# Two unused tiles of 32 bytes that move x, the activations and the weights in SBUF

## The chip, the cores and the metric

The kernel runs on one core of one Trainium2 chip. The metric is the device time in microseconds of one execution. Three timed executions of the kernel before took 531.8, 532.85 and 533.78 us; their median is 532.85 us.

## What is computed

Two steps follow each other: a gated linear attention, and a feed-forward layer with an own activation.

```python
# q, k, v, f_logit: (4, 8, 768, 48) float32
f = 1.0 / (1.0 + np.exp(-f_logit))
state = zeros((B, H, D, D))
for t in range(S):
    state = f[:, :, t, :, None] * state + einsum('bhd,bhe->bhde', k[:, :, t], v[:, :, t])
    y[:, :, t] = einsum('bhd,bhde->bhe', q[:, :, t], state)
x = y.transpose(0, 2, 1, 3).reshape(B * S, H * D)      # 3072 x 384
h = x @ w_in                                           # w_in: 384 x 2048
g = np.where(h >= 1, h, np.where(h <= -1, 0.0, (h + 1) ** 2 / 4.0))
out = g @ w_out                                        # w_out: 2048 x 384
```

## The kernel before, in words

The 768 steps of time are cut into six blocks of 128. In a block the 4 batches lie side by side, so a block has 512 columns. The eight heads are taken as four pairs; a pair of heads lies on 112 of the 128 partitions.

**Attention.** For each block and pair, VectorE builds the running products of the gates with scans and multiplies them into k and q (tile `kq`). TensorE makes the scores (line 411), VectorE masks them (line 417, tile `am`), and TensorE makes the outputs (lines 460 to 465: `am` and `v`, and from the second block on `kq` and the decayed state `dbd`) and the new state (line 493). These matmuls have float32 operands and 128 or 48 columns. ScalarE and VectorE split each output y into a rounded part and the rest, both in the 4-byte type float32r (lines 472 and 473), which is tile `x`: two buffers, one for blocks 0, 2, 4 and one for blocks 1, 3, 5, each of 128 partitions with 2 parts of 3 slices of 512 columns. The rows of the fourth pair go through tile `y3` and small DMAs into `x`.

**Feed-forward layer.** It runs in 96 units: six blocks times 16 slices of 128 of the 2048 inner columns. A unit has three stages:
- nine matmuls of 128x128 weights on 512 columns into PSUM tile `ph` (line 198, function `mm_in`): for each of three slices of x, low weights on the rounded x, high weights on the rounded x, high weights on the rest of x;
- the activation: ScalarE (lines 202 and 205), VectorE (line 210), then its split into `ghi` (ScalarE, line 213) and `glo` (VectorE, line 216);
- nine matmuls into the three PSUM tiles `po` (line 222, function `mm_out`): low weights on `ghi` and high weights on `ghi` for each of three output slices, and then high weights on `glo`.

So there are 1728 matmuls of 512 float32r columns. In each, x, `ghi` or `glo` is the moving operand, which streams through the array, and a slice of `w_hi` or `w_lo` is the stationary operand, which a LDWEIGHTS loads before it. The profile shows the two on rows of their own, PE for the matmul and PEld for the weight load, and the load for the next matmul lies beside the present one.

**Weights.** They come from HBM as 24 pieces of 512 KB (tile `raw`), and in the first 130 us VectorE and ScalarE turn each into a high and a low float32 part (lines 291 to 304, tiles `bits`, `w_hi`, `w_lo`). They stay in SBUF from then on.

**What sets the order.** A planner in the file (class `Plan`) takes every operation with an engine, a cost from a table and what it depends on, simulates the engines and gives out the instructions in the order of the simulated start times. It also puts bf16 matmuls on a tile of zeros (line 272) where it sees TensorE idle for long. Nothing in it knows of addresses.

**Where tiles lie.** All tiles come from one pool with one buffer each. They stand in SBUF in the order in which the code asks for them, each rounded up to a multiple of 32 bytes per partition. Most tiles are a multiple of 64 bytes long; `f`, `kq`, `act` and the small ones are an odd multiple of 32. In the built program before, `x_0` begins at byte 65920 of each partition, `x_1` at 78208, `ghi_0` at 98752, `glo_0` at 102848, `w_hi` at 127424 and `w_lo` at 176576. All six are multiples of 64. Every slice of x that a matmul streams begins a multiple of 2048 bytes further on, every slice of weights a multiple of 512.

Of the kernel before, what the change touches and what calls it, by code (L numbers as in the profile page):

```python
# [10 lines left out]
F32 = mybir.dt.float32  # L11
# [121 lines left out]
def gla_moe(ctx: ExitStack, tc: tile.TileContext, ff, kqd, f0, vv, wd, maskd, identd, gates, values, headsd, out):  # L133
    nc = tc.nc
    const = ctx.enter_context(tc.tile_pool(name="const", bufs=1))
# [3 lines left out]
    def tiles(count, shape, dtype, name):  # L139
        return [const.tile(shape, dtype, name=f"{name}_{k}") for k in range(count)]  # L140
# [11 lines left out]
    kn = tiles(2, [C, B, C], F32, "kn")  # L152
    dbd = tiles(2, [R, B, R], F32, "dbd")
    state = const.tile([R, NP * B, D], F32, name="state")
    x = tiles(2, [128, 2, NP - 1, N], F32R, "x")
    y3 = const.tile([R, 2, N], F32R, name="y3")
    act_f = tiles(2, [128, N + 1], F32, "act")
# [2 lines left out]
    glo = tiles(2, [128, N], F32R, "glo")  # L160
    raw = tiles(4, [128, W], I64, "raw")
    bits = tiles(2, [128, W], U32, "bits")
    w_hi = const.tile([128, 2 * NW, W], F32R, name="w_hi")
    w_lo = const.tile([128, 2 * NW, W], F32R, name="w_lo")
    mask = const.tile([C, C], F32, name="mask")
# [570 lines left out]
```

## Time and profile before

| | |
|---|---|
| timed executions | 531.8, 532.85, 533.78 us (median 532.85) |
| the profiled execution's own time | 534.52 us |
| its span, from the first to the last instruction | 532.7 us |
| mean granted TensorE clock | 0.990 |
| TensorE matmuls busy | 516.1 us, 97% of the span |
| weight loads busy | 407.8 us, 77% |
| VectorE busy | 387.4 us, 73% |
| ScalarE busy | 275.3 us, 52% |
| DMA, mean rate | 78 GB/s |

The profile is one execution. Its views used here are: the page (busy times, the chain of work that ended last by engine and by line), that chain in order of time, the timeline of all instructions in a short window, and groups of instructions by line and shape (number, time in which at least one was running, mean duration of one in ns, idle time ahead of them). Matmuls overlap each other in the records, since one starts to stream while the one before it still drains; so the distance from one start to the next says what a matmul costs, and the mean duration of one is longer. A group in a window contains every instruction that was running in it, so a window of some tens of ns singles out one matmul.

### The profile page before, as it was taken

The page shows a single profiled execution, that of the slowest core. Times are in us where ns is not written, and L with a number is a line of the kernel's source. Part 1 is how long each engine was busy: PE and PEld are TensorE (multiplying, and loading weights), DVE is VectorE, ACT ScalarE, POOL GpSimd, SP SyncE. Part 2 cuts the span into 40 slices and gives each one's busy share as a digit, 9 for nine tenths or more (in the row PEclk, how much of TensorE's full clock was granted, in tenths as well). Part 3 has the DMA queues.
Part 4 walks back from the last instruction along what each step waited for, and adds up shares of the span by engine and source line. Part 5 has one row for each costly group of instructions (what it writes and reads, how often), then busy time and mean ns, then how long its engine had stood idle before and what let it go on. Part 6 is the DMA issues. An engine that isn't in the chain of part 4 may idle for free.

```text
span 532.7 us, 8347 instructions
## 1 busy us (share of the span) xinstructions
PE 516.1 (97%) x3265; PEld 407.8 (77%) x3272; DVE 387.4 (73%) x792; ACT 275.3 (52%) x447; POOL 2.6 (0%) x13
## 2 busy tenths in 40 slices
PE   9996999999999999999999999999999999999994
PEld 4554887778788888878888888888888887888883
DVE  6999899999999999999897697864444343433332
ACT  2589788997443443534534434434433434544442
POOL 1000000000000000000000000000000000000000
PEclk9997999999999999999999999999999999999998
DMA  8684353631332022312023221012300001100001
GB/s 297 207 297 167 120 182 133 218 115 30 95 94 65 19 76 56 99 54 75 22 74 52 84 72 58 1 55 42 93 16 0 2 0 31 61 0 0 1 0 63
DMA packets 18187, 41.67 MB, mean 78 GB/s; under 512 B 2976, under 2 KB 6560, under 8 KB 18144
## 3 DMA queue, kind: packets, MB, share of 16 engines
q1 hardware_dynamic: 18144, 41.09, 24.9%
q8 instruction: 27, 0.44, 0.3%
q14 instruction: 16, 0.13, 0.1%
HBM read 31.63 MB, written 4.72 MB: 68 GB/s over the span
## 4 chain that ended last, share of the span: by engine, by line
PE 78%; DVE 14%; ACT 4%; issue 2%; DMA 0%; SPq 0%; ACTq 0%; DVEq 0%
PE po L222 34%; PE ph L198 32%; PE pa L411 3%; PE pa L465 2%; PE pa L461 2%; PE ph L272 2%; DVE w_lo L304 2%; DVE bits L301 2%; DVE bits L294 1%; DVE act L210 1%; DVE am L417 1%; ACT raw L298 1%; DVE glo L216 1%; PE pa L460 1%; DVE kn L444 1%
## 5 line engine op out<-in xcount | busy, mean ns | idle before, releaser
L198 PE MATMUL ph<-x,w_hi 128*128 128x512 f32 x576 | 181.1, 395 | 0.0
L202 ACT ACTIVATE act<-ph,half 128x512 f32<-128x512 f32 x96 | 65.9, 687 | 151.0 <-PE ph L198 150.2
L198 PEld LDWEIGHTS ph<-x,w_hi 128*128 128x128 f32 x576 | 108.1, 188 | 25.9
L222 PE MATMUL po<-ghi,w_lo 128*128 128x512 f32 x288 | 116.6, 405 | 6.8 <-ACT ghi L213 6.7
L210 DVE SCALAR_TENSOR_TENSOR act<-ph,act 128x512 f32<-128x512 f32 x96 | 65.9, 687 | 75.2 <-ACT act L205 74.6
L198 PE MATMUL ph<-x,w_lo 128*128 128x512 f32 x288 | 114.1, 396 | 0.0
L222 PE MATMUL po<-ghi,w_hi 128*128 128x512 f32 x288 | 114.1, 396 | 0.0
L213 ACT CAST ghi<-act 128x512 fp32r<-128x512 f32 x96 | 59.4, 619 | 67.4 <-DVE act L210 66.9
L222 PE MATMUL po<-glo,w_hi 128*128 128x512 f32 x288 | 83.9, 393 | 0.1
L216 DVE TENSOR_TENSOR glo<-act,ghi 128x512 fp32r<-128x512 f32 x96 | 65.9, 686 | 22.0 <-ACT ghi L213 21.3
L222 PEld LDWEIGHTS po<-ghi,w_lo 128*128 128x128 f32 x288 | 54.4, 189 | 22.5 <-ACT ghi L213 9.2
L198 PEld LDWEIGHTS ph<-x,w_lo 128*128 128x128 f32 x288 | 54.2, 188 | 13.0
L222 PEld LDWEIGHTS po<-glo,w_hi 128*128 128x128 f32 x288 | 54.2, 189 | 12.8 <-DVE glo L216 1.0
L222 PEld LDWEIGHTS po<-ghi,w_hi 128*128 128x128 f32 x288 | 54.5, 189 | 11.9
L205 ACT ACTIVATE act<-act 128x512 f32<-128x512 f32 x96 | 60.7, 632 | 2.9
L444 DVE STREAM_TRANSPOSE kn<-kq 32x128 f32<-32x128 f32 x192 | 58.1, 303 | 2.9
L417 DVE TENSOR_TENSOR am<-pa,mask 128x512 f32<-128x512 f32 x43 | 29.2, 686 | 21.0 <-PE pa L411 17.8
L460 PE MATMUL pa<-am,v 128*64 128x128 f32 x184 | 35.2, 279 | 0.0
L461 PE MATMUL pa<-am,v 128*48 128x128 f32 x184 | 34.5, 276 | 0.1
L465 PE MATMUL pa<-kq,dbd 112*48 112x128 f32 x160 | 30.6, 272 | 0.0
L464 PE MATMUL pa<-kq,dbd 112*64 112x128 f32 x160 | 30.6, 272 | 0.0
L411 PEld LDWEIGHTS pa<-kq 48*128 48x128 f32 x344 | 21.3, 187 | 6.9 <-issue 6.3
(80 smaller groups left out, 478.2 us busy)
## 6 DMA issues: line engine op xcount, KB each, us to landing
raw<-in_w SPq DMA_DIRECT2D x24, 512.0 KB, 4.5
kq<-in_kq SPq DMA_DIRECT2D x18, 512.0 KB, 3.9
v<-in_v SPq DMA_DIRECT2D x24, 192.0 KB, 3.7
out_y<-raw SPq DMA_DIRECT2D x18, 256.0 KB, 2.2
f<-in_f SPq DMA_DIRECT2D x16, 256.5 KB, 2.8
kq<-kq SPq DMA_DIRECT2D x36, 64.2 KB, 2.3
x<-y SPq DMA_DIRECT2D x36, 64.0 KB, 2.3
act<-in_f SPq DMA_DIRECT2D x1, 256.5 KB, 5.5
```

The source lines that it names most:

```text
L198: nc.tensor.matmul(ps, w_in(part, j, kt), xt[:, t, kt], start=(n == 0), stop=(n == 8))
L202: nc.scalar.activation(a, ps, AF.Relu, bias=half, scale=0.5)
L205: nc.scalar.activation(a, a, AF.Square)
L210: nc.vector.scalar_tensor_tensor(out=a, in0=ps, scalar=1.0, in1=a, op0=ALU.max, op1=ALU.min)
L213: nc.scalar.copy(hi, a)
L216: nc.vector.tensor_tensor(out=lo, in0=a, in1=hi.bitcast(F32), op=ALU.subtract)
L222: nc.tensor.matmul(po[e], w_out(part, j, e), g, start=(j == 0 and n == 0), stop=(j == NJ - 1 and n == 2))
L411: nc.tensor.matmul(ps[:, b], kt[a:z, B - 1 - b], qt[a:z, b], start=True, stop=True)
L444: nc.vector.transpose(kn[n % 2][u:u + 32, :, r:r + 32], src[:, :, u:u + 32])
L460: nc.tensor.matmul(ps[0:64, m], vb[:, 0:64], ms[0][:, m], start=True, stop=first)
L461: nc.tensor.matmul(ps[64:R, m], vb[:, D:], ms[1][:, m], start=True, stop=first)
L465: nc.tensor.matmul(ps[64:R, m], dt[:, m, 64:R], qt[:, m], start=False, stop=True)
```

## The change

Two tiles of 128 partitions by 8 float32 (32 bytes per partition) are added to the pool and used by nothing: one just ahead of `x`, the other just ahead of `w_hi`.

```diff
     state = const.tile([R, NP * B, D], F32, name="state")
+
+    const.tile([128, 8], F32, name="apart")
     x = tiles(2, [128, 2, NP - 1, N], F32R, "x")
     y3 = const.tile([R, 2, N], F32R, name="y3")
     act_f = tiles(2, [128, N + 1], F32, "act")
...
     bits = tiles(2, [128, W], U32, "bits")
+    const.tile([128, 8], F32, name="apart_w")
     w_hi = const.tile([128, 2 * NW, W], F32R, name="w_hi")
     w_lo = const.tile([128, 2 * NW, W], F32R, name="w_lo")
     mask = const.tile([C, C], F32, name="mask")
```

The tiles ahead of `x` stay where they were. From `x` to `bits` everything lies 32 bytes higher, and from `w_hi` on 64 bytes higher:

| tile | first byte before | after | before, mod 64 | after, mod 64 |
|---|---|---|---|---|
| `x_0` | 65920 | 65952 | 0 | 32 |
| `x_1` | 78208 | 78240 | 0 | 32 |
| `act_0`, `act_1` | 94592, 96672 | 94624, 96704 | 0, 32 | 32, 0 |
| `ghi_0` | 98752 | 98784 | 0 | 32 |
| `glo_0` | 102848 | 102880 | 0 | 32 |
| `raw_0` | 106944 | 106976 | 0 | 32 |
| `bits_0` | 123328 | 123360 | 0 | 32 |
| `w_hi` | 127424 | 127488 | 0 | 0 |
| `w_lo` | 176576 | 176640 | 0 | 0 |

`y3`, `ghi_1`, `glo_1`, the other buffers of `raw` and `bits` move as their neighbours do; `mask` and `ident`, which stand behind the weights, move by 64. On every engine the instructions, their order and the waits between them are the same before and after; only addresses differ.

## The prediction

> **What bounds the kernel now.** I read the page first: the busy times, then the chain of work that ended last.
>
> ```profile
> PE 516.1 (97%) x3265; PEld 407.8 (77%) x3272; DVE 387.4 (73%) x792; ACT 275.3 (52%) x447; POOL 2.6 (0%) x13
> ...
> PE 78%; DVE 14%; ACT 4%; issue 2%; DMA 0%; SPq 0%; ACTq 0%; DVEq 0%
> PE po L222 34%; PE ph L198 32%; PE pa L411 3%; PE pa L465 2%; PE pa L461 2%; PE ph L272 2%; DVE w_lo L304 2%; DVE bits L301 2%; DVE bits L294 1%; DVE act L210 1%; DVE am L417 1%; ACT raw L298 1%; DVE glo L216 1%; PE pa L460 1%; DVE kn L444 1%
> ```
>
> TensorE is the bound: 78% of the span is its own work, and 66% are the two lines of the feed-forward layer, L198 (x moving) and L222 (`ghi` or `glo` moving). These are the matmuls whose operands move. The chain in order of time gives their price by stage (start in us, length in us, what):
>
> ```profile
> 187.19 2.10 PE ph L198 x9
> 189.29 2.06 PE po L222 x9
> 191.35 2.10 PE ph L198 x9
> 193.45 2.06 PE po L222 x9
> ```
>
> Each stage starts where the one before it ends, so nothing is waited for. Nine matmuls on x take 2.10 us, 233.3 ns each; nine on `ghi` and `glo` take 2.06 us, 228.9 ns each. Is that the least a matmul of 512 columns takes on this chip? The timeline (start, length, engine, line) and a group of two single matmuls say no, for another type:
>
> ```profile
> 38.95 1.03 PE L272 MATMUL ph<-zeros 128*128 128x512 bf16 x4
> ...
> 39.60 0.19 PEld L198 LDWEIGHTS ph<-x,w_lo 128*128 128x128 f32 x1
> ```
> ```profile
> L272 PE MATMUL ph<-zeros 128*128 128x512 bf16 x2 | 0.6, 379 | 0.0
> ```
>
> Four that overlap take 1.03 us, and one alone 379 ns, so one start to the next is (1.03 - 0.379)/3 = 0.217 us. So a float32r matmul on x costs 233.3 - 217 = 16 ns more than a bf16 one of the same shape, one on `ghi` or `glo` 12 ns more. Over the chain that is what an address could win at most. 32% of 532.7 is 170 us, or 81 stages of 2.10 us; 34% is 181 us, or 88 stages of 2.06 us: 81 x 9 x 16 + 88 x 9 x 12 = 11.7 + 9.5 = 21 us. The change is worth as much of these 21 us as hangs on x and the weights standing alike modulo 64, or it costs what the new places bring.
>
> **The change part by part.** No instruction is added, removed or moved, and no wait; the two tiles are written by nobody. Three things get other addresses: the moving operands of L198 and L222 (from 0 to 32 modulo 64), the weights (0 before and after), and what VectorE, ScalarE and the DMAs read and write there.
>
> *The collision of the moving stream with the weight load.* If the 16 and 12 ns came from two reads that meet because both operands stand alike, they would go where no load runs beside the matmul. The trace has such matmuls. With a load beside it (a window at 303.1 us):
>
> ```profile
> L198 PE MATMUL ph<-x,w_lo 128*128 128x512 f32 x1 | 0.4, 394 | 0.0
> L198 PEld LDWEIGHTS ph<-x,w_hi 128*128 128x128 f32 x1 | 0.2, 187 | 0.0
> ```
>
> The last of the nine, which starts 0.23 us later, has no load beside it: the next one is issued only at 303.71 us.
>
> ```profile
> 303.15 0.63 PE L198 MATMUL ph<-x,w_hi 128*128 128x512 f32 x2
> 303.71 0.41 PEld L411 LDWEIGHTS pa<-kq 48*128 48x128 f32 x6 [0.37 <-issue]
> ```
>
> Its group (a window at 303.6 us) shows it alone:
>
> ```profile
> L198 PE MATMUL ph<-x,w_hi 128*128 128x512 f32 x1 | 0.4, 397 | 0.0
> ```
>
> Without a load it took 397 ns, with one 394; the bf16 one took 379. So the extra length is there without the load. The same for `glo` at the program's end, where the last of three starts near 521.25 us and the next load at 521.54:
>
> ```profile
> 520.80 0.84 PE L222 MATMUL po<-glo,w_hi 128*128 128x512 f32 x3
> ...
> 521.54 0.19 PEld L222 LDWEIGHTS po<-ghi,w_lo 128*128 128x128 f32 x1 [0.32 <-ACT ghi L213]
> ```
> ```profile
> L222 PE MATMUL po<-glo,w_hi 128*128 128x512 f32 x2 | 0.6, 388 | 0.0
> ```
>
> 388 ns again, while their distance is (0.84 - 0.388)/2 = 0.226 us. And the other way round: of the four bf16 matmuls above, the last starts at about 39.60 us, beside a load of float32 weights, and stays at 379 ns. The load alone stretches nothing, and the stretch needs no load. I put the gain from keeping them apart at 0, with 21 us as its bound, since the recorded ends of matmuls are modelled and a bf16 stream asks for half the bytes.
>
> The Trainium skill, TensorE: Matmul & The Clock Gate, section "Step-by-step: what each phase is for", says that TensorE reads the moving operand and the weights through two independent ports and that a load takes no bandwidth from the running matmul. By that rule the change saves 0; by the opposite reading up to the 21 us above. The 394, 397 and 379 ns agree with the rule.
>
> *The moving stream's own place.* What then makes 233 of 217 ns? Not one thing that I can name: x costs 233, `glo` 226, and both stand at 0 modulo 64; modulo 128 they differ (x at 0, `glo` at 64), which would fit an effect of the address, but `ghi` stands as `glo` does and is not as even (group means over the whole span):
>
> ```profile
> L198 PE MATMUL ph<-x,w_hi 128*128 128x512 f32 x576 | 181.1, 395 | 0.0
> L222 PE MATMUL po<-ghi,w_hi 128*128 128x512 f32 x288 | 114.1, 396 | 0.0
> L222 PE MATMUL po<-glo,w_hi 128*128 128x512 f32 x288 | 83.9, 393 | 0.1
> ```
>
> No float32r operand stands at an odd multiple of 32 in the trace of before, so the price there is unknown. The nearest rows are the float32 scores of the four pairs of one block, since `kq_0` and `kq_2` begin at even multiples of 32 and `kq_1` and `kq_3` at odd ones:
>
> ```profile
> 208.40 1.09 PE pa L411 x16
> 222.65 1.09 PE pa L411 x16
> 242.97 1.09 PE pa L411 x16
> 263.17 1.09 PE pa L411 x16
> ```
>
> All four take 1.09 us. By them the price is 0, and I take 0. They bind only so far: these streams are slower (16 of 128 columns in 1.09 us, by pairs, against 512 in 233 ns), so a hitch could be hidden. From both sides: the step that the trace has between two places of float32r is 233.3 - 226 = 7 ns. A step down for x, and `ghi` as even as `glo`, is 81 x 9 x 7 + 88 x 9 x 3 = 7 us; a step up for all is (81 + 88) x 9 x 7 = 11 us.
>
> The same page of the Trainium skill, section "Wait — 56ns, not 53.3ns?", gives 215.7 ns from start to start for a warm matmul of 512 columns. By it a unit of 18 would be 3.88 us and no place could make it better; the trace has 2.10 + 2.06 = 4.16 us, so for float32r the measurement decides against the page, and something is left that an address may touch.
>
> *VectorE, ScalarE, DMA.* `act_0` stands at 0 modulo 64 and `act_1` at 32 already; the units use them in turn. ScalarE's first step (single instructions at 459.9, 464, 468 and 472 us):
>
> ```profile
> L202 ACT ACTIVATE act<-ph,half 128x512 f32<-128x512 f32 x1 | 0.7, 687 | 1.4 <-PE ph L198 1.4
> ...
> L202 ACT ACTIVATE act<-ph,half 128x512 f32<-128x512 f32 x1 | 0.7, 689 | 1.4 <-PE ph L198 1.4
> ```
>
> 687 and 689 ns in turn: 2 ns, on an engine that is busy 52%. The DMAs that write `raw` and x get other places too; DMA is 0% of the chain. I count 0 for both.
>
> **The sum.** The profiled execution took 534.52 us, 532.7 of it span; 534.52 + 0 + 0 + 0 = 534.5. It lies 1.67 us above the median of the runs shown, 532.85, as one execution may; the forecast for the median is 532.8.
>
> **Rivals.**
>
> *The stretch is the collision after all.* The recorded ends are modelled, x and the weights are 64 apart modulo 512 while `ghi` and `glo` are not apart from them at all, and x costs more. Against it stand 397 ns without a load and 379 ns beside one. Where it holds, up to 21 us go: 512 us. Not all of it would be kept in the first 200 us, where VectorE is nearly full, so 512 to 517:
>
> ```profile
> 160.00:200.00 40.00, 40.00 (x272) 32.84 (x271) 38.73 (x93) 17.34 (x28) 0.00 (x0) 1.00 0.17 53
> ...
> 300.00:400.00 100.00, 100.00 (x662) 81.73 (x661) 64.34 (x131) 42.92 (x68) 0.00 (x0) 1.00 0.18 53
> ```
>
> (stretch, us, then busy us of PE, PEld, DVE, ACT and POOL, granted clock, DMA share, GB/s: VectorE has 38.73 of 40 us there, 64 of 100 later.)
>
> *The place matters by itself, and the new one is better.* x falls from 233 to the 226 of `glo`. For it: x and `glo` differ in place and in time, and the difference is as regular as the stages' 2.10 and 2.06 us. Against it: `ghi`, and the even 1.09 us. 532.8 - 7 = 526 us.
>
> *The place matters, and the new one is worse* (the other side). A stream of 2048 bytes that starts at 32 modulo 64 covers 33 pieces of 64 bytes where it covered 32. If the moving read works by such pieces, each float32r matmul pays one more step of 7 ns, in all 169 stages of the chain: 532.8 + 11 = 543.5 us. It decides as soon as the step is over 2 ns (169 x 9 x 2 = 3 us). For it: float32r is the one type that is stretched at all, so its read has no slack. Against it: the scores at odd places.
>
> *The change does not do what it says*, because a tile that nobody uses could be left out: the built program has x at 65952 and `w_hi` at 127488, so this one is out.
>
> **How the numbers follow.** Two executions' medians of this kernel can be told apart from about 0.5%, 2.7 us, which is 1.8 ns on each of the chain's 1521 float32r matmuls. No change: 0.44, with its own range of 530.2 to 535.4. The better place: 0.21, the collision: 0.11, together faster 0.32. The worse place: 0.24. The likeliest gives 532.8 us. The range goes down to 520, which leaves out the collision in full and takes in a better place with more than one step, and up to 543.5, one step up.
>
> **What would show it.** If I am right, the chain of the changed kernel still reads 2.10 and 2.06 us a stage and the last matmul on x before the scores 397 ns. Stages near 1.95 us would show the collision, with the lone matmul unchanged at 397; if that one falls too, it was the place. 2.16 us in both stages shows the worse place. ScalarE's 687 and 689 should change places. I am wrong where the stages of L198 and L222 move by over 0.02 us each; a difference of the time with equal stages would have to come from the first 130 us, where VectorE and the DMA of the weights bind.

## The result: 0.6% slower, all of it in the stage on ghi and glo

Ten executions of the changed kernel have a median of 536.19 us (534.75 to 537.18), ten of the kernel before 533.45 us (531.8 to 533.78). The ratio is 1.0057, with a 95% interval of 1.0044 to 1.0071 (this ratio and those below are estimated over all executions and are not quotients of the two medians). The profiled execution has a span of 534.2 us, against 532.7.

The page of the changed kernel (busy us, then the chain of work that ended last by line; the code is three lines longer, so L198 is now L201 and L222 is L225):

```profile
PE 519.0 (97%) x3265; PEld 408.7 (77%) x3272; DVE 387.5 (73%) x792; ACT 275.5 (52%) x447; POOL 2.6 (0%) x13
...
PE po L225 36%; PE ph L201 34%; PE pa L414 4%; PE pa L468 3%; PE pa L464 2%; PE ph L275 2%; DVE w_lo L307 1%; DVE bits L304 1%; ACT raw L301 1%; ACT raw L302 1%; DVE bits L297 1%; PE pa L463 1%; DMA kq<-kq 1%; PE pa L496 1%; ACT bits L303 1%
```

TensorE's matmuls have 2.9 us more of busy time and its weight loads 0.9; the other engines have at most 0.2 us more. The chain in order of time, at the place shown of before:

```profile
187.25 2.10 PE ph L201 x9
189.35 2.10 PE po L225 x9
191.46 2.10 PE ph L201 x9
193.56 2.10 PE po L225 x9
```

The stage on x still takes 2.10 us. The stage on `ghi` and `glo` takes 2.10 instead of 2.06. The recorded lengths of the three kinds of matmul say where (groups over the whole span; before they were 395, 396 and 393 ns):

```profile
L201 PE MATMUL ph<-x,w_hi 128*128 128x512 f32 x576 | 181.1, 395 | 0.0
...
L225 PE MATMUL po<-ghi,w_hi 128*128 128x512 f32 x288 | 114.5, 398 | 0.0
...
L225 PE MATMUL po<-glo,w_hi 128*128 128x512 f32 x288 | 85.6, 399 | 0.1
```

`glo` lost 6 ns a matmul, `ghi` with the high weights 2. A stage can also be measured from the start of its first matmul to the start of the next stage. Averages of this kind, here and below, are taken over the 61 to 66 stages of each sort in which no matmul starts more than 250 ns after the one before it, so that nothing is waited for. Nine matmuls on `ghi` and `glo` took 2060 ns before and 2101 after; nine on x 2100 and 2101. On x the even 233 ns became an uneven row of 226 to 239 ns with the same sum.

How much of the program pays? The same stage of the two kernels, early and late, from the chain of before and then of the changed kernel:

```profile
175.31 2.10 PE ph L198 x9
...
490.42 2.10 PE ph L198 x9
```
```profile
175.30 2.10 PE ph L201 x9
...
492.70 2.10 PE ph L201 x9
```

Up to 175 us the two are level. That VectorE was nearly full until 200 us fits this, but no run tests it as the reason. In the 64 units between the two rows the kernel falls back by 2.29 us, 36 ns a unit, near the 40 ns of the stage. Over the 72 units after 175 us, 36 ns each make 2.6 us; the medians differ by 2.7.

### The profile page after: what moved, and what is told of

The parts are those of the page before. It is cut to its first block, busy times and chain, and to the rows that moved or that the text cites. A ratio compares the mean times of both kernels' runs of the same rounds, so it can differ in the third digit from the quotient of the medians.

```text
span 534.2 us, 8347 instructions
## 1 busy us (share of the span) xinstructions
PE 519.0 (97%) x3265; PEld 408.7 (77%) x3272; DVE 387.5 (73%) x792; ACT 275.5 (52%) x447; POOL 2.6 (0%) x13
## 4 chain that ended last, share of the span: by engine, by line
PE 83%; DVE 8%; ACT 5%; issue 2%; DMA 1%; SPq 0%; ACTq 0%; DVEq 0%
PE po L225 36%; PE ph L201 34%; PE pa L414 4%; PE pa L468 3%; PE pa L464 2%; PE ph L275 2%; DVE w_lo L307 1%; DVE bits L304 1%; ACT raw L301 1%; ACT raw L302 1%; DVE bits L297 1%; PE pa L463 1%; DMA kq<-kq 1%; PE pa L496 1%; ACT bits L303 1%
## 5 line engine op out<-in xcount | busy, mean ns | idle before, releaser
L201 PE MATMUL ph<-x,w_hi 128*128 128x512 f32 x576 | 181.1, 395 | 0.0
L201 PEld LDWEIGHTS ph<-x,w_hi 128*128 128x128 f32 x576 | 108.5, 188 | 26.4
L225 PE MATMUL po<-ghi,w_lo 128*128 128x512 f32 x288 | 118.0, 410 | 6.6 <-ACT ghi L216 6.5
L201 PE MATMUL ph<-x,w_lo 128*128 128x512 f32 x288 | 114.7, 398 | 0.0
L225 PE MATMUL po<-ghi,w_hi 128*128 128x512 f32 x288 | 114.5, 398 | 0.0
L225 PE MATMUL po<-glo,w_hi 128*128 128x512 f32 x288 | 85.6, 399 | 0.1
L225 PEld LDWEIGHTS po<-ghi,w_lo 128*128 128x128 f32 x288 | 54.6, 190 | 22.9 <-ACT ghi L216 8.8
L225 PEld LDWEIGHTS po<-glo,w_hi 128*128 128x128 f32 x288 | 54.4, 190 | 13.9 <-DVE glo L219 1.0
L201 PEld LDWEIGHTS ph<-x,w_lo 128*128 128x128 f32 x288 | 54.2, 188 | 13.3
L225 PEld LDWEIGHTS po<-ghi,w_hi 128*128 128x128 f32 x288 | 54.5, 189 | 11.8
```

The lines of the kernel that those rows point to most:

```text
L201: nc.tensor.matmul(ps, w_in(part, j, kt), xt[:, t, kt], start=(n == 0), stop=(n == 8))
L225: nc.tensor.matmul(po[e], w_out(part, j, e), g, start=(j == 0 and n == 0), stop=(j == NJ - 1 and n == 2))
```

## The experiments

Two theories were set against each other. *Own place*: what a stage costs depends on where its moving operand lies. *Distance*: it depends on the moving operand's address less the weights' address. Distances are given modulo 256 bytes, for a reason that the third experiment shows; before, x has 192 and `ghi` and `glo` have 0; after, x has 160 and they have 224.

### Half the change: the tile ahead of x alone

```diff
+    const.tile([128, 8], F32, name="apart")
     x = tiles(2, [128, 2, NP - 1, N], F32R, "x")
```

> Only the tile ahead of x: x, ghi, glo and the weights all lie 32 bytes higher, so moving operands stand at 32 modulo 64, and their distance to the weights is that of the kernel before. If the moving stream's own place decides: the stage on ghi and glo takes 2.10 us as in the changed kernel, and the time is 536. If the distance between the moving operand and the weights decides: the stages are 2.10 and 2.06 us, x steady at 233 ns, and the time is 533.5.

Measured: 532.46 us against 533.41, ratio 0.9996 (0.9977 to 1.0015). The stages are those of before, 2100 and 2060 ns on average:

```profile
488.57 2.10 PE ph L199 x9
490.67 2.06 PE po L223 x9
492.73 2.10 PE ph L199 x9
494.83 2.06 PE po L223 x9
```

All moving operands are at odd multiples of 32 here, and nothing is lost. Own place is out.

### The other half: the tile ahead of the weights alone

```diff
+    const.tile([128, 8], F32, name="apart_w")
     w_hi = const.tile([128, 2 * NW, W], F32R, name="w_hi")
```

> Only a tile of 32 bytes ahead of the weights: the moving operands stand where they stood before (0 modulo 64), their distance to the weights is that of the changed kernel. Own place: stages of 2.10 and 2.06 us, x steady at 233 ns, 533.5 us. Distance: 2.10 us in both stages, x uneven between 226 and 239 ns, 536 us.

Measured: 536.17 us, ratio 1.0067 (1.0050 to 1.0084), and the stages of the changed kernel:

```profile
487.33 2.10 PE ph L199 x9
489.43 2.10 PE po L223 x9
491.53 2.10 PE ph L199 x9
493.63 2.10 PE po L223 x9
```

Its moving operands lie where they lay before, its distances are those of the changed kernel, and it has the changed kernel's stages down to the average at each of the 18 positions of a unit (within 0.5 ns). The weights' own place is out as well: they begin at the same byte, 127456, here and in the run before, which lost nothing. The distance decides.

### The curve over the distance

Behind the last unit of the kernel before, 64 rows of twelve equal matmuls, with 16 places of x and four of the weights.

```python
for g in (0, 8, 16, 32):                 # weights 0, 32, 64, 128 bytes further on
    for s in range(0, 128, 8):           # x 0, 32, ... 480 bytes further on
        for _ in range(12):
            nc.tensor.matmul(ph[0], wide_w[:, g:g + 128], flat[:, s:s + 512], start=True, stop=True)
```

> The kernel before, with 768 matmuls added behind the last unit whose results nobody uses: for weights that begin 0, 32, 64 and 128 bytes into w_hi, and x taken 0, 32, ... 480 bytes further on, twelve equal matmuls each. Own place: the distance from start to start depends on x's offset alone and is the same in all four groups. Distance: the same curve in the four groups, shifted by 32, 64 and 128 bytes. Values between 226 and 239 ns either way; some 768 x 0.231 = 177 us longer than before.

The same values come back in all four groups, shifted by exactly 32, 64 and 128 bytes, and within each group after 256 bytes. Mean distance from start to start, from the third of twelve on, ns (eight rows for each distance; seven or all eight of them within 0.3 ns of the figure):

| distance modulo 256 | 0 | 32 | 64 | 96 | 128 | 160 | 192 | 224 |
|---|---|---|---|---|---|---|---|---|
| ns | 226.7 | 233.6 | 228.9 | 234.6 | 233.8 | 233.6 | 233.6 | 232.2 |

It is a flat line near 233.6 with two dips, at 0 and at 64. Recorded lengths show the dip too: the group of a window in the row at distance 32 (from 555.9 us), and that of one in a row at distance 0 (from 553.45 us; the windows at distance 0 in the next two parts of the run, from 578.55 and 625.9 us, read the same):

```profile
L612 PE MATMUL ph<-x,w_hi 128*128 128x512 f32 x11 | 2.7, 395 | 0.0
```
```profile
L612 PE MATMUL ph<-x,w_hi 128*128 128x512 f32 x10 | 2.4, 389 | 0.0
```

The kernel before happens to have `ghi` and `glo` at the bottom of a dip. The change moves them out, to 224, and moves x from one place on the flat line to another. In these 175 us VectorE and ScalarE are busy 0.69 and 0.03 us, so no other engine takes part:

```profile
525.20:700.00 174.80, 174.80 (x755) 141.45 (x754) 0.69 (x1) 0.03 (x1) 0.00 (x0) 1.00 0.01 5
```

(stretch, its us, busy us of PE, PEld, DVE, ACT and POOL, granted clock, DMA share, GB/s.)

### Is it the load that takes the time?

Behind the last unit again: loads of 128, 96, 64 and 32 columns, and 512, 384 and 256 moving columns.

```python
nc.tensor.matmul(ph[0][0:cols, 0:n], wide_w[:, 0:cols], flat[:, s:s + n], start=True, stop=True)
```

> The kernel before, with 1008 matmuls behind the last unit whose results nobody uses: equal ones, fourteen in a row, for 32 distances of the moving operand to the weights (8 bytes apart, over 256 bytes) with loads of 128 columns, then for 8 distances (32 bytes apart) with loads of 96, 64 and 32 columns, and with 384 and 256 moving columns. If the stretch is a collision with the load, it goes with the columns loaded: at the distance of x in the kernel before, 16 to 18 ns for 128 columns, 12 to 13 for 96, 8 to 9 for 64, 4 for 32, and it stays at 16 to 18 ns for 384 and 256 moving columns. If it belongs to the moving stream and the load only sets its phase, it stays at 16 to 18 ns for fewer columns loaded, and falls to 12 to 13 and 8 to 9 ns with 384 and 256 moving columns. The fine steps: the dips at distances 0 and 64 modulo 256 are either single points or 32 bytes wide.

Groups of the run, over all distances (after the bar: busy us, mean length in ns):

```profile
L613 PE MATMUL ph<-x,w_hi 128*128 128x512 f32 x448 | 104.6, 395 | 0.0
L613 PE MATMUL ph<-x,w_hi 128*32 128x512 f32 x112 | 26.1, 394 | 0.0
L613 PE MATMUL ph<-x,w_hi 128*96 128x512 f32 x112 | 26.0, 393 | 0.0
L613 PE MATMUL ph<-x,w_hi 128*64 128x512 f32 x112 | 26.0, 393 | 0.0
L613 PE MATMUL ph<-x,w_hi 128*128 128x384 f32 x112 | 19.7, 337 | 0.0
...
L613 PE MATMUL ph<-x,w_hi 128*128 128x256 f32 x112 | 13.4, 281 | 0.0
```

A quarter of the load leaves 394 of 395 ns. From start to start it is 231.9 ns with 128 columns loaded, averaged over the eight distances that the other groups have, and 231.0, 230.6 and 231.3 with 96, 64 and 32. So a load's columns are not what the 16 ns over a bf16 matmul are made of. (The prediction's 217 ns for bf16 came from rounded rows; by the recorded starts, most of its bf16 matmuls in a row stand 215 or 216 ns apart.) With 384 and 256 moving columns it is 174.9 and 118.5 ns. No run has bf16 matmuls of these sizes; three quarters and half of 216 would be 162 and 108, so by this estimate 13 and 10 ns are left: less with fewer columns moved, if not in proportion. The stretch goes with the float32r stream. Yet the dips need the whole load: with 32 columns the values at the eight distances are 230 to 234 ns, and distance 0 (231.6 for x 64 bytes further on) is nothing special. They need all 512 moving columns too: with 384 and 256 of them distance 0 takes 175.6 and 119.5 ns, where the eight distances range over 173.3 to 176.6 and 117.8 to 119.5. In steps of 8 bytes, with 128 columns loaded and 512 moved, the dips are narrow: 230.2 ns at -8, 227.7 at 0, 233.5 at 8; 230.0 at 56, 228.5 at 64, 235.6 at 72. The other places have 230.5 to 240.0, one row each.

### A float32r stream with no float32r load beside it

Behind the last unit: a float32r matmul of x and a bf16 one of zeros in turn.

```python
nc.tensor.matmul(ph[0], wide_w[:, 0:128], flat[:, s:s + 512], start=True, stop=True)
nc.tensor.matmul(ph[1], zeros[:, 0:128], zeros, start=True, stop=True)
```

> The kernel before, with 224 matmuls behind the last unit whose results nobody uses: a float32r matmul of x on w_hi and a bf16 matmul of zeros in turn, fourteen pairs for each of 8 distances (32 bytes apart). Beside the float32r stream runs only the short bf16 load, beside the bf16 stream the float32r load. If the stretch needs a float32r load beside the float32r stream, a pair takes 2 x 217 = 434 ns at every distance. If it belongs to the float32r stream, a pair takes 217 + 227 to 235 = 444 to 452 ns; if the distance to the weights still counts without a float32r load beside it, these differ by up to 8 ns with the distance, otherwise they are equal.

The timeline shows that the two loads go out together, beside the bf16 stream, and that nothing is loaded for a quarter of a us afterwards, while the float32r stream runs:

```profile
530.07 0.10 PEld L612 LDWEIGHTS <-zeros 128*128 128x128 bf16 x1 [0.25 <-issue]
530.07 0.39 PE L612 MATMUL ph<-zeros 128*128 128x512 bf16 x1
530.08 0.20 PEld L611 LDWEIGHTS ph<-x,w_hi 128*128 128x128 f32 x1
530.11 0.58 PE L611 MATMUL ph<-x,w_hi 128*128 128x512 f32 x1
530.53 0.10 PEld L612 LDWEIGHTS <-zeros 128*128 128x128 bf16 x1 [0.25 <-issue]
```

A pair takes 460 to 467 ns, not 434. Some 11 of the 26 to 33 extra ns can be put down to the bf16 matmul's wait for its own weights (390 ns recorded instead of 379). By subtraction 15 to 22 are left for the float32r stream, beside which no load ran; its own record of 0.58 us holds its wait for its turn and can't confirm the split. As far as that goes, it agrees with the prediction that the stretch needs no load. By distance a pair took 460.0 to 466.6, and distance 0 was the longest, not the shortest. So in this order of loads the dip is gone; what it hangs on there isn't settled by this run.

### Other distances in the whole kernel

A tile of 448 bytes ahead of the weights (x at 0, `ghi` and `glo` at 64):

```diff
+    const.tile([128, 112], F32, name="apart_w")
     w_hi = const.tile([128, 2 * NW, W], F32R, name="w_hi")
```

> A tile of 448 bytes ahead of the weights: x now has the distance 0 modulo 512 to the weights that ghi and glo have before, and ghi and glo stand 64 above. Own place: as before, 2.10 and 2.06 us, 533.5. Distance: x takes 227 to 229 ns each, a stage of 2.06 us or less; ghi and glo are at a distance not yet seen, 2.04 to 2.10 us; time 527 to 534.

Measured: 532.23 us, ratio 0.9990 (0.9973 to 1.0007). The stages, 2080 and 2065 ns on average:

```profile
489.17 2.09 PE ph L199 x9
491.26 2.06 PE po L223 x9
493.32 2.08 PE ph L199 x9
495.40 2.06 PE po L223 x9
```

x at distance 0 gains 20 ns a stage, not the 60 that nine times 226.7 promise. Is it the order of low and high weights? Stages of the kernel's own order, behind the last unit, for all pairs of shifts of the low and the high weights:

```python
for a in range(0, 64, 8):                # low weights 0 ... 224 bytes further on
    for b in range(0, 64, 8):            # high weights
        for _ in range(2):
            for kt in range(3):
                for w, c, t in ((w_lo, a, 0), (w_hi, b, 0), (w_hi, b, 1)):
                    at = (3 + kt) * W + 128 + c
                    nc.tensor.matmul(ph[0], flat_of(w)[:, at:at + 128], x[0][:, t, kt], start=True, stop=True)
...
```

> The kernel before, with 2304 matmuls behind the last unit whose results nobody uses: stages of nine as on lines 198 and 222 (same order of low and high weights and of x, ghi and glo), twice each, with the low weights shifted by 0 to 224 bytes and the high ones by 0 to 224 bytes, all 64 pairs. If only the distance modulo 256 of each pair of operands counts, the stage on x takes 9 x 226.7 = 2.04 us where both shifts bring the distance to 0 (a shift of 192 bytes for both), and the stage on ghi and glo takes 2.04 us at shift 0. If the order of the loads counts too (low and high weights in turn), both stay above it, at 2.06 to 2.08 us, as the stage of 2.06 us before and the 2.08 us on x with a tile of 448 bytes suggest.

Measured, the second of two equal stages: with both weights shifted by 192 bytes, distance 0, the stage on x takes 2040 ns, nine times 226.7; with no shift, distance 0 too, the stage on `ghi` and `glo` takes 2045. The other pairs took 2059 to 2124 and 2053 to 2109 ns. So low and high weights in turn cost next to nothing where an equal stage went before. The first of the two equal stages, which follows a stage at other distances, took 2072 and 2078 ns at the same addresses. So what went before counts. In the whole kernel the stage before stands at another distance, and this may be what keeps 2080 from 2040. Then both stages should be short where both stand at 0. That was tried next, with the tiles moved in the kernel itself:

```diff
+    const.tile([128, 16], F32, name="apart")
     x = tiles(2, [128, 2, NP - 1, N], F32R, "x")
...
+    const.tile([128, 48], F32, name="apart_g")
     ghi = tiles(2, [128, N], F32R, "ghi")
```

> A tile of 64 bytes ahead of x and one of 192 bytes ahead of ghi: x, ghi and glo all at distance 0 modulo 256 to the weights. If a stage costs what its distance says: 2.04 us on x and 2.045 us on ghi and glo, a unit 77 ns shorter than the 4.16 us before, over 81 to 88 of the chain's units 6 to 7 us less: 527 us. If a stage also hangs on the order of loads and on the state in which it starts (the kernel with a tile of 448 bytes took 2.08 us on x at this distance): 2.08 and 2.06 us, some 2 us less: 531.5 us.

Measured: 527.42 us against 532.80, ratio 0.9893 (0.9875 to 0.9912), faster than both kernels by more than 1%. The stages average 2041 ns, both of them (nine times 226.7 is 2040):

```profile
487.27 2.04 PE po L224 x9
489.31 2.04 PE ph L200 x9
491.35 2.04 PE po L224 x9
493.39 2.04 PE ph L200 x9
```

And with x at 64 and `ghi` and `glo` at 0:

```diff
+    const.tile([128, 32], F32, name="apart")
     x = tiles(2, [128, 2, NP - 1, N], F32R, "x")
...
+    const.tile([128, 32], F32, name="apart_g")
     ghi = tiles(2, [128, N], F32R, "ghi")
```

> A tile of 128 bytes ahead of x and one of 128 bytes ahead of ghi: x at distance 64 modulo 256 to the weights, ghi and glo at 0. By the distance alone: 9 x 228.9 = 2.06 us on x and 2.045 us on ghi and glo, a unit 55 ns shorter, 528.5 us. If state and order count: at or above 2.08 us on x, 531.5 us or more.

Measured: 531.53 us, ratio 0.9971 (0.9959 to 0.9983). x took 2066 ns, and `ghi` and `glo`, although at distance 0, 2085:

```profile
488.65 2.06 PE ph L200 x9
490.71 2.09 PE po L224 x9
492.80 2.06 PE ph L200 x9
494.86 2.08 PE po L224 x9
```

The stage on `ghi` and `glo` at distance 0 has now cost 2060 ns with x at 192, 2085 with x at 64, and 2041 with x at 0. Its own distance isn't enough: the stage before counts.

### The change's 32 bytes once more, from the best place

The fastest kernel with the change's tile of 32 bytes ahead of the weights:

```diff
+    const.tile([128, 8], F32, name="apart_w")
     w_hi = const.tile([128, 2 * NW, W], F32R, name="w_hi")
```

> The fastest kernel so far (x, ghi and glo at distance 0 to the weights) with 32 bytes ahead of the weights, as the change has them: distance 224 modulo 256 for all. By the curve over the distance: 232 to 233 ns a matmul, 2.10 us in both stages, some 8 us more than without these 32 bytes: 535.5 to 536 us. If only the stage on ghi and glo can lose (as in the change): 2.04 and 2.10 us, 531 us.

Measured: 537.21 us against 532.75, ratio 1.0085 (1.0051 to 1.0119). Both stages are back at 2.10:

```profile
489.14 2.10 PE po L225 x9
491.24 2.10 PE ph L201 x9
493.34 2.10 PE po L225 x9
495.44 2.10 PE ph L201 x9
```

The same 32 bytes that cost 0.6% in the change cost 1.9% here (1.0085 / 0.9893 = 1.019), since here both stages have a dip to lose.

## Why the prediction was wrong

**What bounds the kernel** held: the time moved with the stages of L198 and L222 and with nothing else, and the extra 2.7 us are TensorE's.

**The step that failed** is the first cost: "I put the gain from keeping them apart at 0". It went from a matmul without a load that is as long as one with a load to "the load alone stretches nothing, and the stretch needs no load", and from there to a distance that cannot matter. The first finding holds as far as a load's columns go: a quarter of them left 394 of 395 ns. So does the second: a matmul with no load beside it is longer than a bf16 one. The conclusion doesn't follow. The place of the two operands set the pace by 7 ns a matmul (226.7 at distance 0, 233.6 at 32), and the stage on `ghi` and `glo` went from 2060 to 2101 ns.

Nor could the lone matmul show this. The last matmul on x before the scores, alone in its window, took 397 ns before, and in the fastest kernel, with its next load again issued only after its stream, 388:

```profile
L200 PE MATMUL ph<-x,w_hi 128*128 128x512 f32 x1 | 0.4, 388 | 0.0
```
```profile
300.83 0.19 PEld L200 LDWEIGHTS ph<-x,w_hi 128*128 128x128 f32 x1
301.37 0.30 PEld L413 LDWEIGHTS pa<-kq 48*128 48x128 f32 x4 [0.35 <-issue]
```

From 100 us on, all 23 matmuls on x with no load beside them took 397 ns before, and all 24 in the fastest kernel 388. Their own distance alone does not decide it: in the kernel with 448 bytes ahead of the weights x stands at distance 0 too, and there 19 of 24 took 397 and 5 took 388. One of the 19:

```profile
L199 PE MATMUL ph<-x,w_hi 128*128 128x512 f32 x1 | 0.4, 397 | 0.0
```

So a lone matmul seems to keep what the ones before it were set to (this is inferred from these lengths, not tested), and comparing it with its neighbours in one layout could not show what the layout does. In the changed kernel it stayed at 397, as the prediction asked of its sign (18 of 23; the others 392 or 398), while the stage on L222 moved by 0.04 us, twice the 0.02 that the prediction gave as the sign of being wrong; the one on L198 did not move.

The test that could have been read from the trace of before is the one between layouts: x at distance 192 and `glo` at 0 differ by 7 ns. The prediction saw the 7 ns and tried the moving operand's place modulo 128 for them. Under its first rival it even noted that x and the weights are apart, that `ghi` and `glo` are not, and that x costs more; it gave no price to leaving that place.

**The moving stream's own place** was taken at 0, and is 0: with x, `ghi`, `glo` and the weights all 32 bytes higher the ratio is 0.9996. The even 1.09 us of the scores were a fair sign of it.

**The ceiling of 21 us** was too high as a gain from addresses: the best layout tried won 5.4 us. At distance 0 a float32r matmul still takes 226.7 ns, 11 more than a bf16 one.

**The rivals.** The collision had the right quantity, the distance, with the wrong sign: moving operand and weights at the same place modulo 256 are the fastest pair of all in the rows of equal matmuls, and apart costs up to 8 ns, 7 at most distances. The worse place had the right sign and the right step (7 ns; `glo` lost 6), but for the moving operand's own place and in both stages, 11 us; it was the distance, in one stage of two, and from 175 us on: 2.7. The mechanism that acted, a loss by leaving a good distance, was not in the list.

**ScalarE's 687 and 689** did not change places. They became 692 and 688, on an engine with 1.5 us of idle time ahead of each:

```profile
L205 ACT ACTIVATE act<-ph,half 128x512 f32<-128x512 f32 x1 | 0.7, 692 | 1.5 <-PE ph L201 1.5
```

In the kernel with the tile ahead of the weights alone, where `act` did not move, they are 692 and 688 as well. So they are no sign of `act`'s place.

**The rules of the Trainium skill.** That a load takes no bandwidth from the running matmul (TensorE: Matmul & The Clock Gate, "Step-by-step: what each phase is for") fits the runs with fewer columns loaded, 393 to 395 ns. That the change therefore costs nothing did not follow. The 215.7 ns that the same page of the Trainium skill gives in "Wait — 56ns, not 53.3ns?" agree with the bf16 matmuls (215 or 216 ns) and were reached by no float32r matmul of 512 columns in any layout (224 at least).

## What to carry to other kernels

Where float32r matmuls of 512 columns, with 128 columns of weights each, follow each other without a gap, try moving operands and weights that begin at the same byte modulo 256 in SBUF, in all stages that follow each other; unused tiles are enough, and 64 and 192 bytes were worth 1.1% here. With fewer columns, loaded or moved, the runs show no gain at that place. A layout that is good by chance is lost by any tile that is added between the operands, so print the addresses when a time moves by half a per cent without a reason. And a cost that every matmul of one layout has, with or without a suspected partner beside it, says nothing on what another layout costs: compare layouts.

## What the runs showed of the hardware that was not expected

- A float32r matmul of 512 columns takes 226.7 to 234.6 ns from start to start by the distance of its moving operand to its weights modulo 256 bytes (in steps of 32), with narrow dips at 0 (226.7) and 64 (228.9), in rows of equal matmuls with 128 columns loaded. A bf16 matmul takes 216.
- What is above 216 ns goes with the float32r stream and hardly with the columns loaded: it is 15 to 16 ns with 32 to 128 of them, and by an estimate 13 and 10 with 384 and 256 columns moved. With no load beside it a matmul is still 9 or 18 ns longer than the 379 of a lone bf16 one.
- Stages influence the next: nine matmuls on `ghi` and `glo` at distance 0 took 2041, 2060 and 2085 ns after stages on x at distances 0, 192 and 64, and at unchanged addresses a second equal stage took 2040 where the first took 2072.
- Open: why the loads' addresses set the pace of a stream that doesn't need them, and why the dip at 0 is gone with short loads, with fewer moving columns and with bf16 matmuls between. The runs show where it acts and how much it is, and no more.
